# A spectral filter followed by an ELU network on one Trainium2 core: another opening, with the filter loaded straight into SBUF and the first unit multiplied plainly

## The chip, the cores and the metric

The kernel runs on one core of a Trainium2 chip. The metric is the device time of one execution in microseconds (us); a comparison uses the median of several runs. The engines are named as in the profile: PE is the tensor engine (PEld is its weight load), DVE the vector engine, ACT the scalar engine, POOL the GpSimd engine, SP the sync engine, which here only issues transfers. Beside SP, ACT and POOL issue transfers from their own instruction queues.

## The reference

```python
# x: 8 x 3008 x 256, filt_r and filt_i: 1505 x 256 (float32)
X = np.fft.rfft(x, axis=1)
F = (filt_r + 1j * filt_i)[None, :, :]
y = np.fft.irfft(X * F, n=3008, axis=1).astype(np.float32)
# moe_w_in: 256 x 2048, moe_w_out: 2048 x 256 (they arrive as float64)
x = y.reshape(8 * 3008, 256)
h = x @ w_in
g = np.where(h > 0.0, h, np.exp(np.minimum(h, 0.0)) - 1.0)
return (g @ w_out).astype(np.float32)
```

A filter in the frequency domain along the sequence, for each of 8 batches, and then a two-layer network with ELU between its layers, for all 24064 tokens. All arithmetic of the kernel is in float32.

## The kernel before, in words

**The transform.** The length 3008 is 47 x 64, so the transform is done in two stages of small matrix products, forward and back. For batch 0 this is the opening of the kernel and has functions of its own. `x_load_first(c)` loads one of six pieces of x, with its table from `tf` beside it; `a_first(c)` (L308) multiplies them on PE and copies the result with ACT (L315) into `zt`; `t_first(g)` transposes one of eight groups on PE (L327, copied by ACT, L328); `b_first(g)` does the second stage (L372) and DVE multiplies it with the filter (`products`, L376 to L379); `bi_first(g)` goes back (L372, copied by ACT, L404 and L405); `y_write_first(g)` writes the group to a scratch tensor `yd` in DRAM. `y_read(0, 0)` reads the first part back in another order, and `n_unit(0, 0)` (L552) finishes it on PE. For the batches 1 to 7 the same work is done by `x_load`, `x_unit`, `a_unit`, `z_write`, `z_read`, `f_read`, `b_unit` and so on, spread through the network's steps of the batch before.

**The network.** A unit is a batch `b`, one of six token blocks `m` (448 tokens for m = 0, 512 for the others) and a quarter `q` of the 2048 hidden columns, 192 units in all. A unit's two products go by Strassen's scheme with seven instead of eight block products: seven up steps (L622) into four PSUM banks, DVE additions (L630), ELU on ACT (Relu L639, Exp L640) and DVE (L644), sums on DVE, and, one unit later, seven down steps (L704). The blocks of the weights come with sums of blocks that Strassen's scheme needs (`w_sums`, L846).

**The weights.** They are float64 in DRAM. `w_fetch(k)` loads one of 16 blocks of 512 KB as pairs of 32-bit words, and the kernel makes float32 of them: `w_split(k)` takes mantissa and exponent out of the high word on DVE (L804, L805), `w_float(k)` turns three words into floats on ACT (four activations, L814), `w_join(k)` puts sign, mantissa and exponent together on DVE (L820, L822, L829 or L835). Quarter q needs blocks 4q and 4q+1 for its up steps, 4q+2 and 4q+3 for its down steps. Blocks 0 to 11 are joined in the opening or in the first unit; 12 to 15 in the units 1 and 2.

**The filter.** `f_arrange` copies filt_r and filt_i from DRAM to DRAM (`fd`) in the order that the opening wants, by 28 transfers of POOL's queue; `f_read_first` reads that into `ff` (16 transfers). For the later batches `f_pairs` makes another arrangement, `fp`, out of `fd`.

**What sets the order.** Everything is issued in an order written out by hand: the opening is a straight list, and a table `plan` gives each later step a unit and a place in it (2 after the third step, 3 after the fifth, 0 in the middle, 1 at the unit's end). Each engine's queue is worked off in order. The semaphores that keep buffers and transfers apart are put in when the program is built. For transfers of SP's and ACT's queues there are eight completion counters, handed out in turn; a transfer is issued only when the transfer before it on its counter has landed. POOL's queue has eight of its own.

Of the kernel before, what the change touches and what calls it, by code (L numbers as in the profile page):

```python
# [11 lines left out]
FP32 = mybir.dt.float32  # L12
# [14 lines left out]
P = 128  # L27
# [14 lines left out]
def _make_tables():  # L42
# [27 lines left out]
    tf = np.ascontiguousarray(ta.reshape(P, H, 4, K2).transpose(0, 1, 3, 2)).reshape(P, H, P)  # L70
# [51 lines left out]
    tw = np.ascontiguousarray(tn[:, 0:8].reshape(4, K2, 8, 2, 2, 32).transpose(1, 0, 2, 4, 3, 5)).reshape(P, 8, P)  # L122
# [12 lines left out]
def kernel(  # L135
# [47 lines left out]
    edges = glob.tile([P, 2], FP32, name="edges")  # L183
    unit = glob.tile([P, P], FP32, name="unit")
    fd = fdp.tile([NG, 2, 48, 2, 2, D], FP32, name="fd")
# [107 lines left out]
    def x_load_first(c):  # L293
# [4 lines left out]
        if c < 2:  # L298
            nc.sync.dma_start(tas[0, c], tf_d[:, 4 * c:4 * c + 4, :])
        elif c % 2 == 0:  # L300
            nc.sync.dma_start(tas.pop(("pair", c // 2)), tf_d[:, 4 * c:4 * c + 8, :])
# [16 lines left out]
    def t_first(g):  # L318

        t = t2s[0, g] = t4p.tile([P, 4, D], FP32, tag="t4", name="tf") if g % 4 > 1 else t2[:, g % 4]  # L320
        for j in range(2):
            i = j + 2 * (g % 2 if g < 4 else 0)
            ps = psO.tile([P, 2, 256], FP32, tag="po%d" % i, name="po%d" % i)
            for u in range(2):
                k = 4 * g + 2 * j + u
                for dh in range(2):
                    nc.tensor.transpose(ps[0:ROWS, u, ts(dh, P)], zt[k // 16][dh][:, ts(k % 16, ROWS)], eye)  # L327
# [31 lines left out]
    def f_read_first(g, t):  # L359
        for a, r in enumerate((LO, HI)):  # L360
            nc.gpsimd.dma_start(t[r].rearrange("p c u d -> p (c u d)"), fd[g, a].rearrange("q c u d -> q (c u d)"))
# [12 lines left out]
    def products(re, im, f, sr, si, p, q):  # L374

        nc.vector.tensor_tensor(out=sr, in0=re, in1=f[:, 0], op=ALU.mult)  # L376
        nc.vector.tensor_tensor(out=si, in0=re, in1=f[:, 1], op=ALU.mult)
        nc.vector.scalar_tensor_tensor(out=p, in0=im, scalar=-1.0, in1=f[:, 1], op0=ALU.mult, op1=ALU.mult)
        nc.vector.tensor_tensor(out=q, in0=im, in1=f[:, 0], op=ALU.mult)  # L379
# [144 lines left out]
    def y_read(b, m, *parts):  # L524
        t = t4s[b, m] = t4p.tile([P, 4, D], FP32, tag="t4", name="t4")
        for k in parts or (slice(0, K2),):
            if whole(b, m):
                r = slice(4 * k.start, 4 * k.stop)
                nc.sync.dma_start(t[r], yds[b].rearrange("k (p i) d -> (k p) i d", p=4)[r, 4 * m:4 * m + 4, :])
                continue  # L530
            for r in range(2):
                o = 64 * r
                nc.sync.dma_start(t[o + 2 * k.start:o + 2 * k.stop].rearrange("q i d -> q (i d)"),
                                  yds[b][k.start + r:k.stop:2].rearrange("k (p i) d -> k p (i d)", p=4)
# [606 lines left out]
```

## Time and profile before

| | |
|---|---|
| Median of 3 runs | 2551.64 us (2550.46 to 2552.0) |
| The profiled execution | 2553.3 us, its span 2551.5 us |
| Busy shares of the span | PE 99%, PEld 85%, DVE 83%, ACT 60%, POOL 6% |
| First and last `a_first` matmuls (L308) start | 13.08 and 40.22 us |
| First copy of a transposed group (L328) | 45.34 us |
| First filter product (L376) | 49.48 us |
| Last copy of the way back (L405) ends | 78.09 us |
| First up step of the first unit (L622) | 89.14 us |
| DMA in the first 100 us | 26.91 MB, mean 269 GB/s |

How to read it: the span is the time from the first to the last instruction of one profiled execution. A busy PE is not PE at its peak. From about 140 us on PE has no gaps, so the end of the kernel is set by the time at which the units begin, by the matmuls in them, and by the waits of the first units.

### The profile page before, as it was taken

What the parts mean: (1) busy time and instruction counts of PE and PEld (TensorE: products, weight loads), DVE (VectorE), ACT (ScalarE), POOL (GpSimd) and SP (SyncE); (2) the same over time, 40 slices, a digit from 0 to 9 for tenths busy, and PEclk for the clock granted to TensorE, in tenths of its full rate; (3) what the DMA queues carried; (4) which work ended last, traced back from release to release, by engine and by line L of the source; (5) the groups of instructions that cost most, each with busy time, mean ns of one, the idle gap of its engine ahead of it and who ended that gap; (6) DMA issues with size and microseconds to landing.
All of it is one profiled execution on the core that took longest, in us unless ns stands there. A gap on an engine that the chain in (4) does not pass through costs nothing.

```text
span 2551.5 us, 45225 instructions
## 1 busy us (share of the span) xinstructions
PE 2517.5 (99%) x17266; PEld 2162.0 (85%) x17266; DVE 2112.0 (83%) x3649; ACT 1527.3 (60%) x2680; POOL 159.4 (6%) x315
## 2 busy tenths in 40 slices
PE   6999999999999999999999999999999999999999
PEld 5788889888898888988889888888889888898888
DVE  6878888888788888888888888788897888876766
ACT  6765556655565565565555656555555655555555
POOL 5001000010000000000000000000100010000000
PEclk9999999999999999999999999999999999999999
DMA  9662213422134231433215331243213322120010
GB/s 281 176 183 68 66 36 82 126 68 68 42 99 102 66 70 40 112 87 74 55 40 139 73 80 36 69 125 82 63 41 81 91 61 65 36 46 19 20 28 17
DMA packets 229452, 198.35 MB, mean 78 GB/s; under 512 B 128326, under 2 KB 201558, under 8 KB 229236
## 3 DMA queue, kind: packets, MB, share of 16 engines
q1 hardware_dynamic: 214740, 164.57, 26.2%
q0 software_dynamic: 14000, 30.44, 4.3%
q8 instruction: 136, 2.23, 0.4%
q14 instruction: 80, 0.66, 0.1%
q10 hardware_dynamic: 496, 0.46, 0.1%
HBM read 123.50 MB, written 78.12 MB: 79 GB/s over the span
## 4 chain that ended last, share of the span: by engine, by line
PE 97%; DMA 2%; DVE 1%; SPq 0%; issue 0%; ACT 0%; DVEq 0%
PE po L704 45%; PE phs L622 25%; PE phd L622 13%; PE pha L622 6%; PE psn L574 2%; PE pf L427 1%; PE pv L499 1%; DMA xc<-in_x_dram 1%; PE psa L246 1%; PE po L372 1%; DMA x<-in_x_dram 1%; PE po L327 0%; PE psr L372 0%; PE psa L265 0%; PE psa L308 0%
## 5 line engine op out<-in xcount | busy, mean ns | idle before, releaser
L704 PE MATMUL po<-g,wo 128*128 128x256 f32 (+1 forms) x5376 | 1317.6, 377 | 0.0
L704 PEld LDWEIGHTS po<-g,wo 128*128 128x128 f32 x5376 | 1010.7, 190 | 166.2 <-issue 52.4
L633 ACT ACTIVATE g<-phs 128x512 f32<-128x512 f32 (+1 forms) x576 | 338.8, 588 | 742.9 <-PE phs L622 741.5
L640 ACT ACTIVATE e<-e 128x512 f32<-128x512 f32 (+1 forms) x768 | 477.3, 621 | 24.4
L644 DVE SCALAR_TENSOR_TENSOR g<-e,g 128x512 f32<-128x512 f32 (+1 forms) x576 | 387.4, 673 | 13.6 <-ACT e L640 13.2
L630 DVE TENSOR_TENSOR g<-phd,g 128x512 f32<-128x512 f32 (+1 forms) x384 | 258.9, 674 | 158.1 <-ACT e L640 107.6
L622 PE MATMUL phs<-y,wi 128*128 128x256 f32 (+1 forms) x1536 | 387.6, 375 | 0.0
L622 PE MATMUL phd<-y,wi 128*128 128x256 f32 (+1 forms) x1504 | 380.3, 375 | 0.0
L639 ACT ACTIVATE e<-g 128x512 f32<-128x512 f32 (+1 forms) x576 | 354.4, 615 | 34.2 <-DVE g L630 26.7
L622 PEld LDWEIGHTS phs<-y,wi 128*128 128x128 f32 x1536 | 291.7, 190 | 33.3 <-ACT g L633 0.2
L622 PEld LDWEIGHTS phd<-y,wi 128*128 128x128 f32 x1504 | 284.8, 190 | 35.1 <-DVE g L630 2.7
L644 DVE SCALAR_TENSOR_TENSOR g<-e,phs 128x512 f32<-128x512 f32 (+1 forms) x192 | 129.9, 677 | 115.2 <-ACT e L640 115.2
L622 PE MATMUL phs<-yt,wi 128*128 128x256 f32 (+1 forms) x768 | 193.9, 375 | 0.9 <-ACT g L633 0.9
L622 PE MATMUL phs<-yb,wi 128*128 128x256 f32 (+1 forms) x768 | 193.8, 375 | 0.6 <-ACT g L633 0.6
L622 PE MATMUL pha<-yb,wi 128*128 128x256 f32 (+1 forms) x736 | 185.9, 375 | 0.0
L639 ACT ACTIVATE e<-phs 128x512 f32<-128x512 f32 (+1 forms) x192 | 112.3, 585 | 111.9 <-PE phs L622 111.8
L622 PEld LDWEIGHTS phs<-yt,wi 128*128 128x128 f32 x768 | 145.7, 190 | 17.9 <-ACT g L633 1.4
L622 PEld LDWEIGHTS phs<-yb,wi 128*128 128x128 f32 x768 | 143.9, 190 | 19.3 <-ACT g L633 1.0
L366 POOL DMA_DIRECT2D fall<-fp x224 | 110.1, 499 | 722.1 <-DVE r L472 697.1
L622 PEld LDWEIGHTS pha<-yb,wi 128*128 128x128 f32 x736 | 139.8, 190 | 16.1
L630 DVE TENSOR_TENSOR g<-pha,g 128x512 f32<-128x512 f32 (+1 forms) x192 | 129.3, 673 | 28.3 <-PE pha L622 28.3
L681 DVE TENSOR_TENSOR g<-g,g 128x512 f32<-128x512 f32 (+1 forms) x192 | 130.7, 681 | 6.7
(177 smaller groups left out, 2077.9 us busy)
## 6 DMA issues: line engine op xcount, KB each, us to landing
yd<-t SPq DMA_DIRECT2D x127, 192.0 KB
t<-yd SPq DMA_DIRECT2D x92, 256.0 KB
fall<-fp POOLq DMA_DIRECT2D x224, 96.0 KB, 2.9
t<-z SPq DMA_DIRECT2D x224, 96.0 KB
out_dram<-o SPq DMA_DIRECT2D x624, 32.0 KB
z<-t SPq DMA_DIRECT2D x144, 128.0 KB
xc<-in_x_dram SPq DMA_DIRECT2D x84, 128.0 KB
xc<-in_x_dram SPq DMA_DIRECT2D x161, 64.0 KB
```

The costliest lines, as they stand in the source:

```text
L246: nc.tensor.matmul(ps[k][1][a:a + 32, u, :], w[r, u, 32 * o:32 * o + 32], parts[o][r, u, :], start=True, stop=True, tile_position=(32 * k, a))
L366: nc.gpsimd.dma_start(t[32 * a:32 * a + 24].rearrange("p c u d -> p (c u d)"), fp[g, a].rearrange("q c u d -> q (c u d)"))
L372: nc.tensor.matmul(ps[:, u:u + w, :], table[k, v, :], r[k, u:u + w, :], start=n == 0, stop=n == len(rhs) - 1)
L574: nc.tensor.matmul(o, t[r, i - 4 * m, ds(dh * P + 64 * c, 64)], w[r, i - 4 * m, :], start=True, stop=True)
L622: nc.tensor.matmul(ps[:, a, 0:h], w_in[q][:, COMBO[n], a, :], y[n], start=start and a == 0, stop=True, skip_group_check=True)
L630: nc.vector.tensor_tensor(out=g[o], in0=i0, in1=i1, op=ALU.add)
L633: nc.scalar.activation(out=g[o], in_=i0, func=AXT.Copy)
L639: nc.scalar.activation(out=e, in_=src, func=AXT.Relu, scale=-1.0)
L640: nc.scalar.activation(out=e, in_=e, func=AXT.Exp, scale=-1.0)
L644: nc.vector.scalar_tensor_tensor(out=g[n], in0=es[n], scalar=1.0, in1=src, op0=ALU.subtract, op1=ALU.max)
L681: nc.vector.tensor_tensor(out=b12, in0=b22, in1=b12, op=ALU.subtract)
L704: nc.tensor.matmul(po[i][:, u, 0:h], w_out[q][:, COMBO[n], a, :], g[n][:, a, :], start=q == 0 and a == 0 and n in (1, 3, 6, 4), stop=True, ...
```

## The change

The opening is rewritten. (1) The table `tf` is stored at half its size (64 of 128 columns); `a_table` makes the full table on DVE from it, three operations for each of six pieces, after SP has loaded it into the buffer `t3`. (2) x and the half table come first on SP's queue, ahead of all weights. (3) `f_arrange`, `fd` and `f_read_first` are gone. `f_first` loads the filter from the inputs straight into `ff`, in three parts of frequencies (4, 4 and 8 of 16), and each part by three queues: the forward rows ("f", 24 rows) by SP, the mirrored rows "m" (16 rows) by ACT and "s" (7 rows) by POOL. ACT issues its three batches of four transfers between the copies of `a_first`: after the pieces 1, 3 and 5. `ff` is cleared by POOL instead of ACT and DVE. (4) The weights are all fetched by SP behind the filter, and no block is converted before the last two steps of the loop over the groups: blocks 0 to 5 in the rest of the opening, the others three to a unit in the units 0 to 3, where a `step(k)` is `w_split(k)`, `w_float(k)` and `w_join(k - 1)`; `w_sums` follow in the units 3 to 7 (before: in the opening, one on POOL, and in the units 0, 2 and 3). The conversion has one ACT operation less (three). (5) The first token block (b = 0, m = 0, four units) is multiplied plainly: eight up and eight down steps for each unit instead of seven, no sums of weights or of activations, four ELU blocks that read PSUM. (6) `y_write_first` goes by POOL's queue (ACT's for the last half), and so does `y_read(0, 0)`. (7) The steps of batch 1's first stage move one unit later, (3, 3, 4, 4, 5, 5) instead of (2, 2, 3, 3, 4, 4); `b_unit(1, 0)` stays at the end of unit 6. (8) `f_pairs` reads the inputs instead of `fd`, and the order of the 32 rows in `yd` of batch 0 changes with the order of the filter parts (`t_first`, `tw`, `y_read`).

The core of the diff:

```diff
-    tf = np.ascontiguousarray(ta.reshape(P, H, 4, K2).transpose(0, 1, 3, 2)).reshape(P, H, P)
+    tf = np.ascontiguousarray(ta.reshape(P, H, 4, K2)[:, :, 0::2].transpose(0, 1, 3, 2)).reshape(P, H, 64)
...
-        if c < 2:
-            nc.sync.dma_start(tas[0, c], tf_d[:, 4 * c:4 * c + 4, :])
-        elif c % 2 == 0:
-            nc.sync.dma_start(tas.pop(("pair", c // 2)), tf_d[:, 4 * c:4 * c + 8, :])
+    def a_table(c):
+        t = th[:, XC * c:XC * c + XC]
+        o = tas[0, c].rearrange("p u (k f) -> p u k f", f=4)
+        nc.vector.tensor_copy(out=o[:, :, :, 0:4:2], in_=t)
+        for f, k in ((1, 1), (3, 0)):
+            nc.vector.tensor_scalar(out=o[:, :, :, f], in0=t[:, :, :, k], scalar1=signs, scalar2=None, op0=ALU.mult)
...
-                k = 4 * g + 2 * j + u
                 for dh in range(2):
-                    nc.tensor.transpose(ps[0:ROWS, u, ts(dh, P)], zt[k // 16][dh][:, ts(k % 16, ROWS)], eye)
+                    nc.tensor.transpose(ps[0:ROWS, u, ts(dh, P)], zt[j][dh][:, ts(2 * g + u, ROWS)], eye)
...
-    def f_read_first(g, t):
-        for a, r in enumerate((LO, HI)):
-            nc.gpsimd.dma_start(t[r].rearrange("p c u d -> p (c u d)"), fd[g, a].rearrange("q c u d -> q (c u d)"))
...
+        for c, src in enumerate((filt_r, filt_i)):
+            for a in range(2):
+                o, row, e = 64 * a, 16 * a + k, 1 if k == a == 0 else 0
+                if "f" in parts:
+                    queue.dma_start(ff[o:o + 48:2, c, k:k + n].rearrange("q k d -> q (k d)"),
+                                    raw(src, row, [[64 * D, 24], [1, n * D]]))
+                for j, m, part in ((0, 16, "m"), (16, 7, "s")):
+                    if part in parts:
+                        queue.dma_start(ff[o + 2 * j + 1:o + 2 * (j + m):2, c, k + e:k + n],
+                                        raw(src, 64 * (j + 1) - row - e, [[64 * D, m], [-D, n - e], [1, D]]))
+            if k == 0 and "f" in parts:
+                queue.dma_start(ff[1:48:2, c, 0], raw(src, 32, [[64 * D, 24], [1, D]]))
...
+                (nc.sync if m else nc.gpsimd).dma_start(t[r], yds[b].rearrange("k (p i) d -> (k p) i d", p=4)[r, 4 * m:4 * m + 4, :])
                 continue
...
+    def plain(b, m):
+        return (b, m) == (0, 0)
...
+    def plain_ups(b, m, q):
+        h, y = half(m), ys[b, m]
+        rows = ((y[1], y[7]), (y[2], y[3]))
...
+        def step(i, j, k):
+            if k == 0:
+                held[i, j] = bank("php")
+            n, ps = held[i, j]
+            for a in range(2):
+                nc.tensor.matmul(ps[:, a, 0:h], w_in[q][:, 2 * k + i, a, :], rows[k][j],
+                                 start=k == a == 0, stop=True, skip_group_check=True)
+            if k == 1:
+                src = ps[:, :, 0:h]
+                e = ep.tile([P, 2, 256], FP32, tag="e", name="e")[:, :, 0:h]
+                nc.scalar.activation(out=e, in_=src, func=AXT.Relu, scale=-1.0)
+                nc.scalar.activation(out=e, in_=e, func=AXT.Exp, scale=-1.0)
+                nc.vector.scalar_tensor_tensor(out=g[i, j], in0=e, scalar=1.0, in1=src, op0=ALU.subtract, op1=ALU.max)
+                banks.append(held.pop((i, j))[0])
+        steps = [lambda i=i, j=j, k=k: step(i, j, k) for i, j in BLOCKS for k in range(2)]
...
+    def plain_downs(b, m, q):
+        h = half(m)
+        g = g_of.pop((b, m, q))
...
+        def step(i, j, e):
+            for a in range(2):
+                nc.tensor.matmul(po[e][:, j, 0:h], w_out[q][:, 2 * i + e, a, :], g[i, j][:, a, :],
+                                 start=q == i == j == a == 0, stop=True, skip_group_check=True)
...
-    def w_fetch(k, queue=nc.gpsimd):
+    def w_fetch(k, queue=nc.sync):
         q, j = divmod(k, 4)
...
+        if k in (3, 4, 5, 6):
+            wd = xp.tile([P, 2, 2, D], FP32, tag="xc", name="wd").rearrange("p k u d -> p (k u d)")
+        elif k in (7, 8, 9):
             wd = t1p.tile([P, XC, D], FP32, tag="t1", name="wd").rearrange("p u d -> p (u d)")
...
+        elif k in (12, 13):
+            wd = zq[:, 2 * k - 24:2 * k - 22].rearrange("p a u d -> p (a u d)")
+        elif k in (14, 15):
+            wd = t2[:, k - 14].rearrange("p u d -> p (u d)")
         else:
...
     def w_split(k):
-        m, e, f, l = wts[k] = wtmp[{9: 2, 10: 1, 11: 0, 12: 3, 13: 4, 15: 5}.get(k, k % 2)]
+        m, e = wts[k] = wtmp[k % 3 if k < 10 else (1, 3, 4, 0)[k % 4 - 2]]
...
     def w_float(k, *parts):
-        m, e, f, l = wts[k]
-        ef = e.bitcast(FP32)
-        steps = ((l, wds[k][:, :, 0], AXT.Identity, 2.0 ** -52, 0.0), (f, m, AXT.Identity, 2.0 ** -20, 1.0),
-                 (ef, e, AXT.Relu, -8.0, edges[:, 0:1]), (e, ef, AXT.Relu, -1.0, edges[:, 1:2]))
-        for i in parts or range(4):
+        m, e = wts.get(k, (None, edges.bitcast(U32)))
+        ef, l = e.bitcast(FP32), wds[k][:, :, 0]
+        steps = [(l.bitcast(FP32), l, AXT.Identity, 2.0 ** -52, 1.0),
+                 (ef, e, AXT.Relu, -8.0, edges[:, 0:1]), (e, ef, AXT.Relu, -1.0, edges[:, 1:2])]
+        for i in parts or range(3):
             o, x, func, scale, bias = steps[i]
             nc.scalar.activation(out=o, in_=x, func=func, scale=scale, bias=bias)
...
+    def w_join(k):
         q, j = divmod(k, 4)
-        m, e, f, l = wts[k]
-        if 0 in parts:
-            nc.vector.scalar_tensor_tensor(out=e, in0=wds.pop(k)[:, :, 1], scalar=0x80000000, in1=e,
...
+        w_sign(k)
+        m, e = wts[k]
+        e, f, l = e.bitcast(FP32), m.bitcast(FP32), wds.pop(k)[:, :, 0].bitcast(FP32)
+        nc.vector.scalar_tensor_tensor(out=f, in0=m, scalar=2.0 ** -20, in1=l, op0=ALU.mult, op1=ALU.add)
...
-                for c, s in enumerate((2, 2, 3, 3, 4, 4) if b == 1 else (0, 0, 3, 3, 4, 4)):
+                for c, s in enumerate((3, 3, 4, 4, 5, 5) if b == 1 else (0, 0, 3, 3, 4, 4)):
...
```

The list of the opening and the plan of the conversions as they stand after the change (they replace the ones printed above):

```python
            for c in range(2):
                nc.gpsimd.memset(ff[:, c], 0.0)
...
            nc.sync.dma_start(flat_th[:, 0:2 * XC], tf_d[:, 0:2 * XC])
            for c in range(NXC):
                x_load_first(c)
...
            nc.sync.dma_start(once, once_d)
            nc.sync.dma_start(gs, gs_d)
            parts = ((0, 4), (4, 4), (8, 8))
            for k, n in parts:
                f_first(k, n, "s", nc.gpsimd)
                f_first(k, n, "f", nc.sync)
            tn_read(0, 0)
            for k in range(3):
                w_fetch(k)
...
            for c in range(NXC):
                a_table(c)
            for c in range(NXC):
                a_first(c)
                if c % 2 and c < 5:
                    f_first(*parts[c // 2], "m", nc.scalar)
            f_first(*parts[2], "m", nc.scalar)
            for k in range(3, 6):
                w_fetch(k)
            for g in range(4):
                t_first(g)
            for g in range(NG + 2):
                back = (lambda g=g: bi_first(g - 2)) if g >= 2 else None
                if g < NG:
                    b_first(g, [ff[:, c, 2 * g:2 * g + 2] for c in range(2)], pqs[g % 2], back)
                else:
                    back()
                if g < 4:
                    t_first(g + 4)
                if g >= 2:
                    y_write_first(g - 2, (nc.gpsimd, nc.scalar if g == NG + 1 else nc.gpsimd))
                if g >= NG:
                    step(g - NG)
...
            y_read(0, 0, slice(0, K2 - 4), slice(K2 - 4, K2))
            for k in range(6, 10):
                w_fetch(k)
            step(2)
            for k in range(10, 16):
                w_fetch(k)
            for k in range(3, 6):
                step(k)
            warm = psO.tile([P, 512], FP32, tag="po2", name="warm")
            for k in range(7):
                nc.tensor.matmul(warm, w_in[0][:, 0, 0, :], w_in[0][:, 0:2].rearrange("p a b c -> p (a b c)"),
                                 start=True, stop=True)
...
        def step(k):
            if k < 16:
                w_split(k)
                w_float(k)
            w_join(k - 1)
        for quad, place, fn, k in ((0, 2, step, 6), (0, 0, step, 7), (0, 1, step, 8), (1, 2, step, 9), (1, 0, step, 10), (1, 1, step, 11),
                                   (2, 2, step, 12), (2, 0, step, 13), (2, 1, step, 14), (3, 2, step, 15), (3, 0, step, 16),
                                   (3, 1, w_sums, 1), (4, 2, w_sums, 3), (4, 1, w_sums, 5), (5, 2, w_sums, 7), (5, 1, w_sums, 9),
                                   (6, 2, w_sums, 13), (6, 1, w_sums, 11), (7, 1, w_sums, 15)):
            at(quad, place, fn, k)
```

## The prediction, made before the changed kernel ran

> **What bounds the kernel now.** I read the page first, then the chain of waits, then the windows, then SP's waits.
>
> The page gives the span, the busy shares and the shares of the chain:
>
> ```profile
> span 2551.5 us, 45225 instructions
> ...
> PE 2517.5 (99%) x17266; PEld 2162.0 (85%) x17266; DVE 2112.0 (83%) x3649; ACT 1527.3 (60%) x2680; POOL 159.4 (6%) x315
> ...
> PE 97%; DMA 2%; DVE 1%; SPq 0%; issue 0%; ACT 0%; DVEq 0%
> ```
>
> PE is busy in 2517.5 of 2551.5 us, so only 34 us lie outside its work, nearly all of them in the opening and the first units. The change can therefore move the end in three ways: it moves the start of the units, it changes PE's own work, or it makes PE wait inside the early units.
>
> The chain of waits, start and length in us, shows what the opening runs on:
>
> ```profile
> 3.20 10.88 DMA xc<-in_x_dram
> 14.09 13.14 DMA xc<-in_x_dram
> 27.25 12.84 DMA x<-in_x_dram
> 40.22 3.77 PE psa L308 x16
> 44.54 3.82 PE po L327 x31
> ...
> 70.89 6.08 PE po L372 x46
> 78.12 2.66 DMA yd<-t
> 80.86 3.68 DMA t<-yd
> 84.55 1.26 issue
> 85.80 3.56 PE psn L552 x16
> ```
>
> Until 40 us it is x that arrives between other loads; from 44.5 to 78 us the group loop on PE; then y's way over DRAM. The first up step (L622) is at 89.14.
>
> The windows (start:end, length, busy us of PE, PEld, DVE, ACT, POOL, then PE's clock, DMA share, GB/s):
>
> ```profile
> 0.00:20.00 20.00, 5.25 (x23) 5.02 (x24) 13.99 (x26) 16.18 (x22) 12.52 (x27) 1.00 0.93 268
> 20.00:40.00 20.00, 12.47 (x59) 11.48 (x58) 9.81 (x21) 11.59 (x26) 8.01 (x14) 0.87 1.06 334
> ...
> 100.00:120.00 20.00, 18.33 (x104) 17.98 (x103) 18.82 (x36) 14.50 (x26) 0.00 (x0) 1.00 0.31 95
> 120.00:140.00 20.00, 19.39 (x144) 16.78 (x143) 19.03 (x36) 14.93 (x26) 0.52 (x1) 1.00 0.56 159
> ...
> 500.00:1000.00 500.00, 500.00 (x3443) 426.17 (x3443) 431.49 (x737) 296.67 (x520) 31.70 (x63) 1.00 0.28 68
> ```
>
> DMA is full for the first 40 us (5.36 MB, then 6.68 MB). DVE carries 86% of every later unit (431.49 of 500), and where it reached 95% (100 to 140 us, 37.85 of 40) PE lost 2.28 us. Two waits of SP's queue (us in total, times, longest) show a queue that stands for an earlier transfer of its own kind, which it does not need as data:
>
> ```profile
> SPq L297 <- DMA xc<-in_x_dram: 3.3, 3, 2.3
> SPq L794 <- DMA tn<-tf_t: 2.2, 1, 2.2
> ```
>
> These are the completion counters: the ninth transfer waits for the first. On SP this costs little, as nothing but transfers stands behind it.
>
> **The change part by part.**
>
> **x first.** x with the half table is 3.87 MB, the other early loads of SP (small tables, f, tn) 2.21 MB. At the first window's 268 GB/s x is there at 14 to 16 us instead of 40. Six pieces at 3.75 us (rows of L308, all cold) could then end near 28. The three DVE operations of `a_table` for each piece lie beside 3.75 us of PE work, and DVE was busy for 13.99 of the first 20 us with work that is now later: nothing on the path; without that cover, one table ahead of the first piece, about 1.6 us (512 columns and twice 256, by rows of 0.69 and 0.42).
>
> **The m batches on ACT.** Here the order of the built program speaks. Behind the copies of pieces 0 and 1 (L315, now L319), ACT's queue holds this:
>
> ```
> 10 L372 DMACopy ff_119<-in_filt_r_dram 16x3x256 [waits DMAHW6_49,Pool_49]
> 11 L372 DMACopy ff_119<-in_filt_r_dram 16x4x256 [waits DMAHW7_49]
> 12 L372 DMACopy ff_119<-in_filt_i_dram 16x3x256 [waits DMAHW1_49,Pool_49]
> 13 L372 DMACopy ff_119<-in_filt_i_dram 16x4x256 [waits DMAHW4_49]
> 14 L319 Activation zt0_125<-psa_251 128x16x2x8 [waits PE_49]
> ```
>
> Each waits on a counter that it shares with SP. The last transfers on those counters are tn and the weight blocks 0, 2 and 3 (second half), which SP issues after all x, tables and f. ACT works in order, so the copies of piece 2 stand behind weight block 3, those of piece 4 (second batch) behind block 6, and the copies of the transposes (third batch) behind block 8. Through block 3 there are 8.7 MB on the way, through block 6 10.5, through block 8 11.8. With 5.36 MB in the first 20 us and 0.31 to 0.334 MB per us after it, plus about 2 us from the last byte to the counter (y's small transfer took 2.66 in all), the batches are through at 30 to 33, 37 to 39 and 41 to 43 us. The blocks from 3 on go into buffers of x and of tables, so they also wait for PE's pieces, and a faster load would not end the hold by itself. The first copy of a transposed group stood at 45.34; I put it at 43: **-2.3**. So the early x buys next to nothing.
>
> **The group loop** took from 45.34 to 78.09 (last L405, start 77.50 and 0.59). Conversions leave it: about 3.5 us of DVE and 13 us of ACT (L814 rows). What remains is PE: 64 transposes at 0.123 (31 in 3.82) and the L372 matmuls, some 25 to 27 us, with ACT's copies (0.50 each) beside. I take 29.8 instead of 32.8: **-3**; bounds 0 and -6.
>
> **Behind the loop.** y went out and back in 2.66 and 3.68 us with 1.26 of issue. Now POOL issues the read, at about 0.55 us instead of 0.45, and ACT has the floats of blocks 1 to 5 ahead of the y copy, three operations or 0.57 + 1.38 = 1.95 us each, 9.75 in all, against 7.6 us (2.66, 3.68, 1.26) of round trip that hide them: **+1.8**, bounds 0 and +5. Together S, the start of the units, is -3.5 (near 85.6), bounds -8 and +1.
>
> **The plain unit.** Four units of 16 steps instead of 14 are 8 more steps. A step of 224 columns in the rows of L622 and L704 is 0.757 us: **+6.06**, on PE, so on the path, with nothing to hide it. The DVE work that it saves (sums of activations, L630, L680 to L684) is spent below.
>
> **Units 0 to 3.** Before, they took 49.3 us (89.14 to 138.41), of which steps are 49 x 0.757 = 37.1, the first L552 1.8 and two batches of L265 3.8: 6.6 of waiting. Now PE has 37.1 + 6.06 + 1.8 + 1.9 = 46.9 (one L265 batch has moved out). Three blocks are converted in each unit; on the path ACT, DVE, ACT a block of ELU and a block of conversion take turns: Relu 0.60, Exp 0.58, max 0.54, split 0.67, two floats 1.38 and the hand-overs, about 3.9, three times, and a fourth ELU block of 1.15: 12.9 per unit, 51.6 in four. That leaves 4.7 of waiting, and about 1 more at three units whose first step needs a block just joined (L820, L822: 0.60 and 0.66): 7.7, so **+1.1**, bounds -4 and +4.
>
> **Units 3 to 8.** The eight `w_sums` (L846, four operations in 1.62 us) come into ordinary units: 13 us of DVE. Five units are 64 us on PE (2551.5 - 89.1 over 192.25 units is 12.8) and 1.9 of L265; DVE has 86.3% of 64, 55.2, and 13: 68.2. It is over by 2.3, and the loss of the 100-to-140 window at 95% (2.28 in 40) adds 3.8: 6.1 at least. At most, each of the eight stands in front of a max for which PE's banks wait: 13. I take **+8**. Batch 1's first stage ends one unit later while `b_unit(1, 0)` stays: from the last L265 copy (152.67) over z's write and read (landed near 167) the way was 14.3, and with the transposes behind it needs some 18.4; 14.0 are left from the end of unit 5. Up to 4.4, I take **+2**, as the slow unit 6 covers part. These waits together, W, are +11; bounds 0 and +21.
>
> **Sum.** -3.5 + 6.06 + 11 = +13.6, on the profiled 2553.3: 2566.9. The median lies 1.7 below the profiled execution, so 2565.2; I say 2566.
>
> The Trainium skill ("DMA: Bandwidth & Descriptors", section "Issuing engines are not separate DMA queues") says that all issuing engines end at the same 16 DMA engines, and that issuing from several only saves sequencer time. By that rule the twelve transfers given to ACT save SP about 5.4 us of issue and nothing else. The windows agree that the DMA engines were already full (shares 0.93 and 1.06).
>
> **The rivals.**
>
> A, the sum above. For it speaks the built order, against it that a sum of waits is soft.
>
> B, the conversion and the sums are covered. In plain units DVE loses its sums, and the banks let PE run ahead. Then W is about 1: -3.5 + 6.06 + 1, 2555. Against it: DVE is at 86% even in late units.
>
> C, the other side: ACT is not held. If the three batches are issued as ACT reaches them (their counters free before), the copies follow PE, the first transposed group is copied near 28 instead of 43 (the sixth piece's end, above), and S is -18.5. With W at 1.1 + 2.3, the bare surplus of DVE, that is -18.5 + 6.06 + 3.4 = -9: 2543. It decides when the hold ends 13.6 us earlier than I put it. Against it: SP's two waits, which show the counters at work.
>
> D, slower transfers. The filter now goes in pieces of 24, 16 and 7 rows of 1 to 8 KB, and no row of before shows such shapes into SBUF. If the load runs at 268 GB/s throughout, the 11.8 MB are there at 44 and the third batch at 46: +3; with z's trip at its full 4.4 and the sums at 13: +13.6 + 3 + 2.4 + 5 = 24, 2576.
>
> A rule of the Trainium skill bears on D ("DMA: Bandwidth & Descriptors", section "Why a DMA increments its semaphore by 16 and not by 1"): a transfer uses as many engines, up to 16, as divide its slowest dimension. By it 24 rows would use 12 engines; the 1.62 MB of f at three quarters of the rate is an estimated 1.7 us more. No row of before shows it.
>
> **How the numbers follow.** A 0.68, B 0.14, C 0.08, D 0.10. About 0.2% (5.1 us) is what a measurement of this kernel can tell from no change. Faster by more is C: 0.08. Within it lie half of B and a sliver of A: 0.08. Slower: 0.84. The range: S's and W's bounds seldom meet, so 11 us around A, 2555 to 2577, taking in B; upward D's own bounds (2576 and 7), so 2583.
>
> **What would show it.** Right: ACT's transfers of L372 at 26 to 33, 36 to 39 and 42 to 43 us, with ACT idle before the copies of pieces 2 and 4; the first copy of a transposed group (L328, now L331) near 43; the first plain step near 85.6; units 0 to 3 in 56 to 58 us; DVE at 95% in units 4 to 8. Wrong: a first L331 copy before 35, units 4 to 8 gapless on PE, or the finishing matmuls of later blocks (L574, now L593) late by another amount than 14 us.

## The result, and the profile after

The changed kernel takes 2581.76 us (median of 4 runs, 2577.43 to 2582.66) against 2551.05 us beside it: a ratio of 1.011 (95% interval 1.0096 to 1.0123), 30.7 us slower. The forecast was 2566, +14; the range (2555 to 2583) holds the result near its upper end, and the move is twice the forecast.

The page of the changed kernel, the same three lines as before:

```profile
span 2580.9 us, 45255 instructions
...
PE 2527.1 (98%) x17298; PEld 2169.5 (84%) x17298; DVE 2099.4 (81%) x3633; ACT 1508.0 (58%) x2651; POOL 152.6 (6%) x291
...
PE 95%; DMA 2%; DVE 1%; ACT 1%; SPq 1%; issue 0%; ACTq 0%; POOL 0%; DVEq 0%; POOLq 0%
```

PE's busy time grew by 9.6 us, the span by 29.4, so PE also idles about 20 us more. The trace, cut at the forecast's own marks, shows where (us):

| stretch | before | after | change | forecast |
|---|---|---|---|---|
| to the first copy of a transposed group (L328, now L331) | 45.34 | 49.30 | +4.0 | -2.3 |
| group loop, to the end of the last L405 (now L420) | 32.75 | 32.81 | +0.1 | -3 |
| behind the loop, to the first up step (L622, now L639) | 11.05 | 16.13 | +5.1 | +1.8 |
| units 0 to 3 | 49.27 | 59.94 | +10.7 | +5.3 (6.06 - 1.9 + 1.1) |
| from unit 4 (158.18 us) to the end | 2413.1 | 2422.7 | +9.6 | +11.9 (1.9 + 8 + 2) |

The first three rows are the forecast's S: +9.1 instead of -3.5.

ACT's timeline shows the hold (start, length in us, engine, line, operation, out<-in, shapes, and in brackets the idle time before it and what ended it):

```profile
17.86 0.38 ACT L319 ACTIVATE wo<-psa 128x256 f32<-128x256 f32 x1
32.88 2.60 ACTq L372 DMA_DIRECT2D ff<-in_filt_r_dram  x2
36.91 2.81 ACTq L372 DMA_DIRECT2D ff<-in_filt_i_dram  x2
39.76 0.38 ACT L319 ACTIVATE zt<-psa 128x256 f32<-128x256 f32 x1 [21.52 <-DMA ff<-in_filt_r_dram]
...
49.30 2.06 ACT L331 ACTIVATE t<-po 112x512 f32<-112x512 f32 x4 [1.12 <-PE po L330]
```

Between the copies of piece 1 and of piece 2 ACT stands still for 21.5 us. (The bracket names ACT's own transfers; what held these shows in the chain below.) Its four transfers go out at 32.9 to 39.7 us, and only then do the copies of pieces 2 and 3 run, which PE needs to go on.

The chain of waits after, in the parts that answer to the chain before (start, length):

```profile
11.19 10.28 DMA x<-in_x_dram
...
22.25 0.72 SPq L368
...
31.07 7.51 DMA wd<-in_moe_w_out_dram
38.60 5.96 DMA wd<-in_moe_w_out_dram
...
80.76 3.81 DMA yd<-t
85.29 6.61 DMA t<-yd
91.90 2.80 issue
```

The last byte of x lands at 21.5 us. From there to 31.0 us the chain is SP itself, which issues one transfer behind the other without a gap, 0.72 us for each of the filter's forward pieces (L368). Then the chain runs through two loads of weights that nothing needs yet, and that is the price of the shared counters. At the end the first part of y's read takes 6.61 us by POOL's queue. The 2.80 behind it are the second part: 64 KB, issued at 87.59 us and landed 7.0 us later, just ahead of L568 at 94.70. Before, SP's read took 3.68 and 1.26 us of waiting behind it.

The windows of the first 40 us (columns as before; the third and fourth cut smaller pieces out of the second):

```profile
0.00:20.00 20.00, 10.02 (x53) 9.72 (x54) 9.27 (x23) 3.92 (x9) 15.16 (x22) 1.00 0.96 212
20.00:40.00 20.00, 1.46 (x14) 1.27 (x12) 0.00 (x0) 0.24 (x1) 0.00 (x0) 0.62 0.89 264
24.00:28.00 4.00, 0.00 (x0) 0.00 (x0) 0.00 (x0) 0.00 (x0) 0.00 (x0) 0.62 0.61 177
36.00:40.00 4.00, 0.00 (x0) 0.00 (x0) 0.00 (x0) 0.24 (x1) 0.00 (x0) 0.50 1.07 374
```

The load is slower than before (268 and 334 GB/s). In the first 20 us the DMA engines are full (0.96) and move only 212 GB/s. From 24 to 28 us, when SP sends little but the 24-row pieces of the filter, 177 GB/s move at a share of 0.61; from 36 to 40 us the load, mostly weight blocks, moves 374 at 1.07. The hold is long for three reasons: what it waits for stands last, x ahead of it arrives slowly, and between 21.5 and 31 us the load goes no faster than SP issues it (181 GB/s at a share of 0.73, with SP's issuing on the chain).

### The profile page after: what moved, and what is told of

It is laid out like the page before. It is cut to its first block, busy times and chain, and to the rows that moved or that the text cites. A ratio compares the mean times of both kernels' runs of the same rounds, so it can differ in the third digit from the quotient of the medians.

```text
span 2580.9 us, 45255 instructions
## 1 busy us (share of the span) xinstructions
PE 2527.1 (98%) x17298; PEld 2169.5 (84%) x17298; DVE 2099.4 (81%) x3633; ACT 1508.0 (58%) x2651; POOL 152.6 (6%) x291
## 4 chain that ended last, share of the span: by engine, by line
PE 95%; DMA 2%; DVE 1%; ACT 1%; SPq 1%; issue 0%; ACTq 0%; POOL 0%; DVEq 0%; POOLq 0%
PE po L786 44%; PE phs L702 25%; PE phd L702 12%; PE pha L702 6%; PE psn L593 2%; PE pf L442 1%; PE pv L514 1%; PE psa L246 1%; PE po L662 1%; PE php L639 1%; DMA wd<-in_moe_w_out_dram 1%; PE po L386 0%; DMA xc<-in_x_dram 0%; DMA x<-in_x_dram 0%; DMA t<-yd 0%
## 5 line engine op out<-in xcount | busy, mean ns | idle before, releaser
L786 PE MATMUL po<-g,wo 128*128 128x256 f32 (+1 forms) x5264 | 1293.1, 378 | 2.3 <-DVE wo L930 2.3
L786 PEld LDWEIGHTS po<-g,wo 128*128 128x128 f32 x5264 | 989.5, 190 | 168.5 <-issue 51.7
L713 ACT ACTIVATE g<-phs 128x512 f32<-128x512 f32 (+1 forms) x564 | 332.2, 589 | 741.7 <-PE phs L702 740.2
L720 ACT ACTIVATE e<-e 128x512 f32<-128x512 f32 (+1 forms) x752 | 467.9, 622 | 23.8
L724 DVE SCALAR_TENSOR_TENSOR g<-e,g 128x512 f32<-128x512 f32 (+1 forms) x564 | 379.9, 674 | 13.6 <-ACT e L720 13.3
L710 DVE TENSOR_TENSOR g<-phd,g 128x512 f32<-128x512 f32 (+1 forms) x376 | 253.7, 675 | 155.9 <-ACT e L720 107.2
L702 PE MATMUL phs<-y,wi 128*128 128x256 f32 (+1 forms) x1504 | 380.0, 375 | 0.0
L702 PE MATMUL phd<-y,wi 128*128 128x256 f32 (+1 forms) x1488 | 376.6, 376 | 0.0
L719 ACT ACTIVATE e<-g 128x512 f32<-128x512 f32 (+1 forms) x564 | 347.6, 616 | 33.3 <-DVE g L710 26.4
L702 PEld LDWEIGHTS phs<-y,wi 128*128 128x128 f32 x1504 | 285.6, 190 | 33.0
L702 PEld LDWEIGHTS phd<-y,wi 128*128 128x128 f32 x1488 | 281.8, 190 | 35.1 <-DVE g L710 2.7
L724 DVE SCALAR_TENSOR_TENSOR g<-e,phs 128x512 f32<-128x512 f32 (+1 forms) x188 | 127.4, 678 | 113.7 <-ACT e L720 113.7
L702 PE MATMUL phs<-yb,wi 128*128 128x256 f32 (+1 forms) x752 | 190.1, 375 | 0.9 <-ACT g L713 0.9
L702 PE MATMUL phs<-yt,wi 128*128 128x256 f32 (+1 forms) x752 | 190.0, 375 | 0.0
L702 PE MATMUL pha<-yb,wi 128*128 128x256 f32 (+1 forms) x736 | 185.9, 375 | 0.0
L702 PEld LDWEIGHTS phs<-yb,wi 128*128 128x128 f32 x752 | 140.9, 190 | 19.5 <-ACT g L713 1.3
L702 PEld LDWEIGHTS phs<-yt,wi 128*128 128x128 f32 x752 | 142.8, 190 | 16.5
L702 PEld LDWEIGHTS pha<-yb,wi 128*128 128x128 f32 x736 | 139.8, 190 | 16.1
L710 DVE TENSOR_TENSOR g<-pha,g 128x512 f32<-128x512 f32 (+1 forms) x188 | 126.7, 674 | 30.4 <-PE pha L702 30.4
```

The lines of the kernel that those rows point to most:

```text
L702: nc.tensor.matmul(ps[:, a, 0:h], w_in[q][:, COMBO[n], a, :], y[n], start=start and a == 0, stop=True, skip_group_check=True)
L710: nc.vector.tensor_tensor(out=g[o], in0=i0, in1=i1, op=ALU.add)
L713: nc.scalar.activation(out=g[o], in_=i0, func=AXT.Copy)
L719: nc.scalar.activation(out=e, in_=src, func=AXT.Relu, scale=-1.0)
L720: nc.scalar.activation(out=e, in_=e, func=AXT.Exp, scale=-1.0)
L724: nc.vector.scalar_tensor_tensor(out=g[n], in0=es[n], scalar=1.0, in1=src, op0=ALU.subtract, op1=ALU.max)
```

## The experiments

### What held ACT

First run: the m transfers go by POOL's queue.

```diff
-                f_first(k, n, "s", nc.gpsimd)
+                f_first(k, n, "sm", nc.gpsimd)
...
-                if c % 2 and c < 5:
-                    f_first(*parts[c // 2], "m", nc.scalar)
-            f_first(*parts[2], "m", nc.scalar)
```

> The twelve m transfers of the filter go by POOL's queue, behind its s transfers, instead of ACT's. Theory (ACT is held: its queue stood 21.5 us from 18.2 to 39.8 us and 3.8 us from 42.1 to 45.9, for the counters that it shares with SP's weights): ACT copies each piece as PE ends it, the first copy of a transposed group (L331) comes near 31 us instead of 49.3 (last byte of x at 21.5, three pieces of some 3 us), the filter is there by then, and everything behind moves by as much: 2582 - 18 = 2564 us (2560 to 2570). Rival (the load itself is slow: 212 and 264 GB/s in the first two windows of 20 us): the copies come early but the products wait for the filter, the first product stays within 5 us of its place, and the time within 2577 to 2583.

Measured: 2559.03 us (2556.04 to 2560.44), ratio 1.0026 (1.0015 to 1.0037). The first L331 copy stands at 26.42 instead of 49.30, the first up step at 75.18 instead of 98.24, and 22.7 us of the 30.7 are gone, a little more than the theory gave. The rival falls: the first product stands at 30.59 instead of 53.21, and what it waited for is PE, not the filter. The loop now takes 36.05 us instead of 32.81, with a write of y on its chain that needs 6.38 us to land, and the way behind the loop is shorter by 3.4.

That run changes the engine and the counters at once. The second leaves the transfers on ACT, where they were, and moves only the later fetches in the written order, so that the counters they share are those of early transfers:

```diff
-            tn_read(0, 0)
-            for k in range(3):
-                w_fetch(k)
...
-            for k in range(3, 6):
+            tn_read(0, 0)
+            for k in range(6):
                 w_fetch(k)
```

> The changed kernel with one move in the written order: tn_read and the fetches of the weight blocks 0 to 2 stand behind the six pieces of x and the three m batches instead of ahead of them. ACT still issues the twelve m transfers between its copies, but their counters are now those of early x and filter transfers. Theory (the counters held ACT, not the issuing): ACT is held until 20 us at most by the first batch and shortly by the others, the first copy of a transposed group comes at 27 to 33 us, and the time is 2560 (2556 to 2568). Rival (twelve issues of 0.6 us each and the transfers' own slowness hold ACT): the first such copy stays after 40 us, 2574 or more.

Measured: 2565.49 us (2564.56 to 2568.37). ACT issues the same twelve transfers:

```profile
25.38 0.38 ACT L319 ACTIVATE zt<-psa 128x256 f32<-128x256 f32 x1 [4.75 <-DMA ff<-in_filt_r_dram]
...
31.57 2.06 ACT L331 ACTIVATE t<-po 112x512 f32<-112x512 f32 x4 [2.56 <-DMA ff<-in_filt_i_dram]
```

The longest hold is 4.75 us instead of 21.5, though it ends at 25.4 and not at 20 us as expected. So at least 16.3 of the 22.7 us are the counters. The other 6.4 go with having the transfers on ACT at all, and the counters have a part in these too, the other way round. Of SP's waits in the first 45 us the longest is that of its last piece of x, for one of ACT's transfers, which it does not need as data:

```profile
SPq L297 <- DMA ff<-in_filt_r_dram: 6.3, 1, 6.3
```

That piece is issued at 21.0 us (11.2 in the changed kernel), and PE then waits 3.78 us for x.

### y by SP again

```diff
-                    y_write_first(g - 2, (nc.gpsimd, nc.scalar if g == NG + 1 else nc.gpsimd))
+                    y_write_first(g - 2, (nc.sync, nc.scalar if g == NG + 1 else nc.sync))
...
-                (nc.sync if m else nc.gpsimd).dma_start(t[r], yds
+                nc.sync.dma_start(t[r], yds
```

> y of batch 0 is written and read back by SP's queue again (the last half of the last group by ACT's, as it is). Theory (the tail behind the loop is 16.3 us instead of 11.1 because POOL's read takes 6.6 us and 2.8 more until L568 starts, where SP's took 3.7 and 1.3): the first L568 starts 4 us earlier and the time is 2578 (2576 to 2580). Rival (the six blocks of floats on ACT, L899, end at 94.2 us and stand ahead of the y copy): L568 is earlier but the first plain step moves by under 1 us, 2581 to 2583. A third: y's writes on SP stand behind weight transfers that wait for their buffers, then slower than 2583.

Measured: 2579.29 us (2578.28 to 2579.6). The first L568 starts at 91.02 instead of 94.70, the first up step at 94.90 instead of 98.24. About 3 us of the tail's 5.1 are gone, as the theory has it. The time moves by 2.5 us, and the two kernels' runs overlap. The cause is open in part: in SP's queue y's read also stands ahead of the weight blocks from 6 on, which now go out from 86.1 us. In the changed kernel the blocks 10 to 15 go out from 82.5 us, beside the read. So this run does not separate POOL's queue from the load beside the read.

### The plain first unit undone

```diff
     def plain(b, m):
-        return (b, m) == (0, 0)
+        return False
...
         n_unit(0, 0)
+        n_sums(0, 0)
```

The weight sums are placed ahead of their first use: two in the opening, six in units 0 to 3.

> The first token block goes by Strassen's scheme again (28 steps of seven blocks fewer: 8 steps less on PE), with the weight sums moved ahead of their first use: two in the opening, six in the units 0 to 3. Theory (the plain unit costs its 8 steps, 8 x 0.757 = 6.06 us, and its waits come from the conversion, which stays): PE's work falls by 6.06, the sums and the scheme's own additions (10 operations a unit instead of 4, some 3.2 us) load DVE in the units 0 to 3 to more than 100%, so half of the gain is lost there, and the units 4 to 8 win 5 us of waits: 2576 (2571 to 2581). Rival (the plain unit is what lets DVE convert three blocks a unit): the units 0 to 3 get longer by more than 6 us than they are now (59.7 us), 2583 to 2592.

Measured: 2596.31 us (2595.18 to 2597.61), 14.5 slower than the changed kernel: the rival, and more than it gave. The units 0 to 3 take 71.98 us instead of 59.94. Waits of PE in the units 0 to 3 (engine, line, releaser: us in total, times, longest), first of this run, then of the changed kernel:

```profile
PE phs L702 <- ACT g L713: 10.8, 4, 3.6
PE pha L702 <- DVE wi L915: 5.0, 1, 5.0
PE phd L702 <- DVE g L710: 3.0, 2, 2.2
```

```profile
PE php L639 <- DVE wi L915: 3.0, 1, 3.0
PE php L639 <- DVE g L646: 2.7, 1, 2.7
PE psn L568 <- DVE g L646: 0.9, 1, 0.9
PE psa L265 <- DVE g L646: 0.3, 1, 0.3
```

18.8 us of waits against 6.9, and the granted clock is 0.86 instead of 0.93. DVE is busy for 66.25 of these 71.98 us, against 43.35 of 59.94. Of the 22.9 us more, some 9.7 are the six sums that this run puts there (1.62 us each), the rest is the scheme's own work; the run does not separate the two. With three conversions to a unit both do not fit beside them, and the plain steps (6.06 us) buy more than they cost here. Whether they also would in a unit without conversions, no run tried.

### The conversion as a chain

On top of the run with m on POOL, the split of each block stands one block earlier:

```diff
-                w_split(k)
                 w_float(k)
+            if k < 15:
+                w_split(k + 1)
             w_join(k - 1)
```

> The m transfers on POOL as in the run before (2559 us), and of each conversion the DVE split (L888, L889) stands one block earlier, so that ACT's floats never wait for it. Theory (the conversion is a chain between ACT and DVE; ACT waited 0.79 us for the split in each of ten blocks in the units 0 to 3, and stands in front of the next ELU): 6 us less, 2553 (2550 to 2555). Rival (PE waits at the starts of units for the last join, 3.0 us, and for bank and ELU, 2.7 and 0.9; these do not come from the split): at most 2 us less, 2557 to 2560.

Measured: 2553.85 us (2549.9 to 2557.71), 5.2 less than the run it starts from; its runs spread over 7.8 us. In the traces the units begin 3.3 us later (78.50 instead of 75.18), and the units 0 to 3 shrink from 58.81 to 52.53 us. ACT's waits for the split, 8.1 us in ten, are gone, and so the split was on the path. PE's waits fall by only 3.3 us with it: those of 2.7 and 0.9 for DVE's ELU are gone, the one of 3.0 for a join stays. The other 3.0 us are PE's own work, 49.22 instead of 52.18 us at a granted clock of 0.98 instead of 0.94.

### The sums and the later stage

Four runs belong together. The sums on POOL (on the changed kernel):

```diff
-            nc.vector.tensor_tensor(out=o, in0=x, in1=y, op=op)
+            nc.gpsimd.tensor_tensor(out=o, in0=x, in1=y, op=op)
```

> The eight weight sums (four operations of 0.42 us on DVE each) go to POOL, where the row of before had 0.73 us for one. Theory (DVE is the late engine in the units 4 to 8; PE waited 2.0 us for L710 there and 2.3 us for the sums L930 themselves, 5.1 us in all): DVE is 13.6 us lighter, PE's waits from 180 to 225 us shrink to 1 to 3 us, 2578 (2575 to 2581). Rival (PE waits for sums that come later still on POOL, 2.9 us for each instead of 1.7, and POOL's clearing and transfers stand behind them): no change or slower, 2581 to 2588.

Measured: 2589.39 us (2585.68 to 2590.65), 7.6 slower. The longest PE wait on L710 grew from 2.0 to 4.4 us: beside POOL's sums (0.72 to 1.17 us each) DVE's own operations take longer (L230 0.859 us instead of 0.684, L724 0.806 instead of 0.684), and 2.2 us of waiting for `t<-yd` are new.

The sums left out, with their blocks cleared by POOL:

```diff
-                                   (3, 1, w_sums, 1), (4, 2, w_sums, 3), (4, 1, w_sums, 5), (5, 2, w_sums, 7), (5, 1, w_sums, 9),
-                                   (6, 2, w_sums, 13), (6, 1, w_sums, 11), (7, 1, w_sums, 15)):
+                                   ):
```

> The changed kernel without its eight weight sums in the units 3 to 7 (the blocks that they would write are cleared by POOL in the opening instead, so this part of the computation is left out). It prices the sums by themselves. Theory (they load DVE beyond what PE leaves it, the +8 of the prediction): 2574 us (2571 to 2576), and PE's waits between 180 and 225 us (2.0, 0.5, 0.9 and 1.7 us) fall under 2 us together. Rival (they lie in DVE's own gaps, DVE has 12 to 15 of 17 us busy per unit there): 2579 to 2583.

Measured: 2584.77 us (2582.18 to 2587.07), not faster but 3 slower, against both my theories. The units began 1.8 us later (100.07). Of that, 1.4 us stand already at the first L331 copy (50.67), as in the last run of these four with the same clearing (50.53); the rest does not come again there, where the units begin at 97.59. From unit 4 on there was nothing won either (2424.4 us against 2422.7). PE's waits from 160 to 235 us name what took their place:

```profile
PE psn L593 <- DMA t<-yd: 3.4, 2, 2.6
PE phd L702 <- DVE g L710: 2.0, 1, 2.0
PE phs L702 <- ACT g L713: 0.3, 1, 0.3
```

The waits for sums are gone, and PE comes early to batch 1's y, which is still on its way.

The early stage alone (on the run with m on POOL):

```diff
-                for c, s in enumerate((3, 3, 4, 4, 5, 5) if b == 1 else (0, 0, 3, 3, 4, 4)):
+                for c, s in enumerate((2, 2, 3, 3, 4, 4) if b == 1 else (0, 0, 3, 3, 4, 4)):
```

> The m transfers on POOL as in the run before (2559 us), and batch 1's first stage where it was before the change, in the units (2, 2, 3, 3, 4, 4) instead of (3, 3, 4, 4, 5, 5). The prediction gave the later place 2 us for z's round trip. Theory: no PE wait on z was seen after the change (the first L442 batch at 201.5 us follows its neighbours without a gap), so nothing is won, and the x units' DVE work (8 operations of 0.69 us a pair) meets the conversions in unit 2: 2560 to 2564. Rival (z's trip or the crowd of sums and x units in the units 4 to 6 is what costs): 2554 to 2557.

Measured: 2557.85 us (2555.24 to 2560.35), 1.2 less, with overlapping runs and between the two expectations: inconclusive.

Both together, on the changed kernel:

> The changed kernel without its weight sums (cleared by POOL in the opening instead, so that part of the computation is left out) and with batch 1's first stage in the units (2, 2, 3, 3, 4, 4). Without the sums alone PE waited 0.8 and 2.6 us for batch 1's y from DRAM (t<-yd, before L593) in place of the 5.1 us it lost to DVE and ACT. Theory (the sums' cost is real, but the stage moved one unit later puts the same time into y's way; with both removed neither wait stands): 2578 us (2575 to 2580), no wait of L593 on t<-yd. Rival (the loss behind unit 4 has another source, PE's own work or the clock): 2581 to 2586.

Measured: 2573.81 us (2573.09 to 2579.39), 8.0 less, more than the theory gave. From unit 4 to the end it takes 2414.1 us (before the change 2413.1), and PE waits for nothing between 158 and 235 us. So 8.6 of the 9.6 us behind unit 4 are the sums and the late stage. Of these, 1.96 are one L265 batch, which the late stage had moved there; it is back in the units 0 to 3, which take 60.31 us with it (59.94 without). Each of the two hides the other: removing the sums alone won nothing, and the stage alone, on the other kernel, next to nothing.

### A version that beats both

Three steps. The first has m on POOL, y read by SP, half of `ff` cleared by ACT, the splits and floats of blocks 0 to 2 inside the loop, blocks to 8 behind the loop, splits ahead, sums one unit earlier.

```diff
+            nc.scalar.memzero(ff[:, 1])
...
-            for k in range(3, 6):
+            for k in range(3, 10):
                 w_fetch(k)
...
+                if 2 <= g < 5:
+                    w_split(g - 2)
+                    w_float(g - 2)
```

> A version that should be nearer to the best: m transfers on POOL, y read back by SP, half of the filter's buffer cleared by ACT, splits and floats of the weight blocks 0 to 2 inside the loop over the groups, all blocks to 8 behind the loop, so seven instead of ten in the units (three a unit in 0 and 1, one in 2), splits ahead, the sums one unit earlier. By the theory that the units 0 to 4 pay for conversions and sums (units 0 to 3 took 58.8 us in the run with m on POOL against 49.3 before, of which 5.3 is plain steps): 2548 us (2543 to 2553). If instead the plain unit's steps and the loop's waits for y's writes are what holds, 2555 to 2560.

Measured: 2548.19 us (2546.31 to 2551.19), ratio 0.9985 (0.9975 to 0.9994). PE now waits 3.74 us for the y copy behind ACT's floats, so the second step puts that copy ahead:

```diff
         n_unit(0, 0)
+        w_float(7)
+        w_split(8)
+        w_join(6)
```

> The version before (2548 us), with the copies of y (L569) ahead of the floats of blocks 7 and 8, and the units' conversions one place later (eight blocks in the units 0 to 2 instead of seven). In that version PE waited 3.74 us at 72.26 us for the y copy, which stood behind ACT's floats, while y had been finished on PE by 68.5. Theory: the first plain step comes at 68 to 69 us, and the units 0 to 3, which had no PE wait there, keep their 50.3 us or lose one: 2545 us (2542 to 2547). Rival (ACT and DVE were at 97% in the window of 80 to 100 us; what leaves the tail comes back as waits in the units 0 to 2): 2547 to 2550.

Measured: 2544.7 us (2542.88 to 2546.48), ratio 0.9968 (0.9956 to 0.9981). The third step is the one-line change of the stage shown above:

> The version before (2544.7 us) with batch 1's first stage in the units (2, 2, 3, 3, 4, 4). There the conversions end in unit 2 and DVE had 13.5 of 20 us busy from 100 to 120 us, so the x units find room. Theory: the wait of 1.5 us for batch 1's y (t<-yd at 187) goes, as in the run without sums and with the early stage, and the others (2.0 and 1.6 us, DVE and ACT under the sums) stay: 2543 us (2540 to 2545). Rival (the x units push the conversions of unit 2 in front of unit 3's first steps): 2545 to 2549.

Measured: 2540.18 us (2538.42 to 2541.06), ratio to the kernel before 0.9955 (0.9941 to 0.9968): 11.5 us faster. It starts the units at 71.81 us (before 89.14) and pays back 3.1 us in units 0 to 3 and 2.0 behind them. The stage that was worth 1.2 us under crowded units is worth 4.5 here (3.3 by the two ratios), more than its theory gave it: besides the wait for y the one of 2.0 us for DVE is gone, which the theory left standing.

## Why the prediction was right and where it was not

**Right in direction and in the main mechanism.** The hold of ACT by counters, read from the built order, was there in the order forecast: batches through at 39.7, 45.8 and 49.2 us, copies waiting behind them. The early x bought nothing, as forecast. The plain steps are eight more, 6.06 us at full clock. That the range holds the time is partly luck. Rival A's own margin ends at 2577; the rest up to 2583 was D's. Of D's terms the load was too small (+3, where the first transposed copy came 6.3 us late) and the sums with the stage too large (17.4, where 7.7 were measured). And one of the prediction's own signs of being wrong came: the finishing matmuls of later blocks (L593) stand 29.1 us later than before and not 14 (196.60, now 225.66).

**The step that failed: S.** It was put at -3.5 with bounds -8 and +1, and measured +9.1. Three terms were mis-sized. (a) The hold, forecast through at 30 to 33, 37 to 39 and 41 to 43 us, ended 6 to 7 us behind the late end each time. I took the rates of the windows before (5.36 MB in 20 us, then 0.31 to 0.334 MB per us) for a load of other pieces; it moved 4.2 and 5.3 MB. x, forecast for 14 to 16 us, landed at 21.5. And the sum had no term for SP's issuing, on which the chain then runs for 9.5 us. That the early load is slow was rival D's place; it should have been in A. (b) The loop's -3 did not come. The conversions that left it had lain in gaps that the loop has anyway: 32.75 us with them, 32.81 without, and 35.43 us in the first step of the best version, which put three splits and floats back into the loop, against 36.05 in the run with m on POOL. No run moved the conversions alone. (c) The tail: POOL's read was costed by its issue (0.55 instead of 0.45) and the landing left as SP's; the landings were 6.61 and 7.0 instead of 3.68. Whether the queue or the weights beside the read did that is open.

One reading of the rows was wrong without effect: the six pieces were not all at 3.75 us, two of the L308 rows of before have 3.42 and 3.04. In the changed kernel two pieces in a row (L312) took 4.12 together.

**Units 0 to 3.** The waits were sized well (7.7 forecast, 6.9 measured). PE's own work was not: busy for 53.01 us, where the sum had 46.9, so 6.1 more. The sum had no term for the clock. The windows of the four units, before and after:

```profile
89.14:138.41 49.27, 45.45 (x281) 41.21 (x281) 45.44 (x87) 36.17 (x65) 0.52 (x1) 1.00 0.55 154
```

```profile
98.24:158.18 59.94, 53.01 (x277) 49.82 (x277) 43.35 (x87) 42.18 (x71) 0.00 (x0) 0.93 0.37 106
```

The granted clock fell from 1.00 to 0.93, an estimated 4.2 us of 59.94 (0.07 of it), the larger part of the 6.1. The forecast also contradicted itself: the sum gave 54.6 us for these units (46.9 and 7.7), the list of signs 56 to 58.

**From unit 4 on.** 11.9 forecast, 9.6 measured: right in size and, by the run without both, in what causes it. The mechanism given for the sums is not borne out: DVE was to be over its limit, at 95% in the units 4 to 8. It was busy for 84% from 160 to 260 us (before 87%). PE's 5.2 us of waits there were for single operations: 2.3 for the sums themselves (L930), 2.0 for DVE's L710, 0.9 for ACT's L713. And I added the sums and the late stage as independent terms (8 and 2); they are two covers over the same stretch.

**The rivals.** B (conversion and sums covered) is out: 6.9 us of waits in units 0 to 3, and 8 us for the sums and the stage. C's mechanism is real, since without the hold the kernel gains 22.7 us; its sign is not, because units 0 to 3 still took 58.8 us (before 49.3) and the rest 2424.7 (2413.1), where C had given W only 3.4. D's slow load happened, but that the shape of the pieces is its cause is not shown; its size for z's trip was not seen as such.

**The two rules.** The Trainium skill's rule that issuing from several engines only saves sequencer time ("DMA: Bandwidth & Descriptors", "Issuing engines are not separate DMA queues") agrees with the runs: taking the twelve transfers off ACT lost nothing and gained 22.7 us. But the sequencer's time is not small here: SP's issuing is on the chain for 9.5 us. The Trainium skill's rule on how many engines a transfer uses ("DMA: Bandwidth & Descriptors", "Why a DMA increments its semaphore by 16 and not by 1") gives 12 of 16, 0.75, for 24 rows; the window with little but these shows 0.61. SP was issuing there without a gap, so the share may be that of its pace, and no run separates the two.

## What to carry to other kernels

Before a transfer is given to a second engine's queue, look at what else is in that queue and which earlier transfer its completion counter belongs to: an engine that computes can be held by a load that it does not need. Cost a moved load at the rate of its own pieces, not at the rate of the window it moves into, and count the time that its queue takes to issue it. When two terms cover the same stretch, take both away in one run before calling either free.

## What the runs showed of the hardware that I had not expected

**A wait of two or three us can cost PE its clock, and need not.** Steps of four matmuls behind a wait (at full clock 0.76 us from start to start for L639 and L662, 0.86 for L702 and L786). In the changed kernel:

```profile
140.94 1.81 PE L639 MATMUL php<-y,wi 128*128 128x224 f32 x4 [2.98 <-DVE wi L915]
142.54 1.70 PE L662 MATMUL po<-g,wo 128*128 128x224 f32 x4
```

From 140.94 to 144.99 us three steps take 4.05 us instead of 2.27, at a granted clock of 0.58. So the wait of 2.98 costs 4.8. In the run with the splits ahead the same wait costs hardly more than itself; the clock behind it is 1.00:

```profile
115.46 1.02 PE L639 MATMUL php<-y,wi 128*128 128x224 f32 x4 [2.98 <-DVE wi L915]
116.32 0.92 PE L662 MATMUL po<-g,wo 128*128 128x224 f32 x4
```

In the run with the y copy first a wait of 1.98 us is enough, and the clock is 0.51 from 146.48 to 149.56 us:

```profile
145.51 1.13 PE L702 MATMUL phd<-yb,wi 128*128 128x256 f32 x4 [1.98 <-DVE g L710]
146.48 1.82 PE L786 MATMUL po<-g,wo 128*128 128x256 f32 x4
```

In the changed kernel the same wait, at 185.40 us, left the clock at 1.00. So the length of the wait alone does not decide; what does, no run shows. The Trainium skill ("TensorE: Matmul & The Clock Gate", section "HAM oscillation — how this bites in real kernels") puts the limit at idle gaps over about 3.4 us; here 1.98 was enough in one run, and 2.98 was not in another.

**POOL's clearing stops DVE.** While POOL cleared `ff` (two operations of 3.6 us), DVE's first table copy (L303) took 2.02 us instead of 0.29 and two L305 3.78 instead of 0.53, each ending within 0.3 us behind one of POOL's. In the last version, where POOL clears only half of `ff` in one such operation, L303 still took 1.94 us and the two L305 behind it 0.52. The Trainium skill ("SBUF — State Buffer", section "SBUF: two separate sides") describes such an exclusive lock between the two engines; the durations agree with it.
